# Maxima of the first attention unit from unstacked halves of queries and keys, in 32-row tiles

## The chip, the cores and the metric

The kernel runs on one core of a Trainium2 chip. The metric is the device time of one execution in microseconds (us), lower is better. The times before the change are 1361.73, 1362.64 and 1366.7 us, median 1362.64.

## The reference

Two independent parts, their outputs side by side (448 columns each), sequence length 2048, all in float32. Part A is a state-space convolution (a kernel made of complex exponentials, and a long convolution by Fourier transforms). Part B, which the change touches, is full attention with 16 heads of 28 elements:

```python
qkv = (x @ wqkv).reshape(B, S, 3, H, Dh).transpose(2, 0, 3, 1, 4)
q, k, v = qkv[0], qkv[1], qkv[2]
p = softmax(einsum("bhqd,bhkd->bhqk", q, k) * Dh ** -0.5)
o = einsum("bhqk,bhkd->bhqd", p, v)
return o.transpose(0, 2, 1, 3).reshape(B, S, D) @ wo
```

## The kernel before

**Precision.** TensorE's fast float32 form rounds its operands. So queries, keys, inputs and weights are split in a rounded high half and the rest, hi and lo (`hl` in the names), and a product is the sum of products of halves. Each head is padded from 28 to 32 rows. For the scores, hi and lo are *stacked*: `load_q` (line 162) copies a unit's queries from DRAM into a tile `qhat` with 128 rows, hi, hi, lo, lo; `load_k` (line 143) copies a head's keys into a tile `khat` with hi, lo, hi, lo. One matmul with 128 rows then gives all four products at once.

**Units and maxima.** Attention runs in 16 units, each four heads (a group) by 512 queries. A unit needs the maximum of each query's scores before its exponentials. `max_mm` (line 170) makes, for each of 16 pairs of head and block of 128 queries, four products of 512 keys. The first two blocks of keys are taken as a difference (`kdif`, of the first and second halves of key blocks) and the second halves: max(a, b) = relu(a - b) + b. ScalarE makes the relu (tile `rl`) of the first product, VectorE adds the second and reduces in one instruction, and reduces the third and fourth products alone; all go to the tile `mx`. `max_join`, `max_end` and `max_put` (lines 191 to 206) join them, transpose them, and write them negated as two more rows into the unit's `qhat`, so that score products (`pss`) come out shifted.

**Stages.** In the first stage (about 250 us), 48 projection jobs (`qk_proj`, line 447, and `v_proj`) run among the "seeds" of part A, which load VectorE, ScalarE and POOL (GpSimd); `project` (line 519) takes one job, and the slots of lines 527 to 540 place jobs and the loads named in `ahead`. A projection is 12 matmuls into a PSUM tile `pm` (three of them rotate); its evacuation makes hi on ScalarE and lo on VectorE into a tile `hl` (two rotate), and stores both halves to DRAM (`k<-hl`, `q<-hl`). At the end of that stage the buffers of weights (`w_p`) and inputs (`y_p`) are closed (`wst.close()`), the four `khat` of the first group are loaded into the room, eight of the sixteen loads from ScalarE's queue and eight from SP's, then the second unit's `qhat` and the values `v`, and the maxima of the first unit follow (lines 543 to 548), 64 products into five PSUM tiles. Then comes the long loop. It starts with three steps of the second unit's maxima (`LEAD`, line 860), and goes on with score products, exponentials, products with the values, further maxima, and the rest of part A.

**Order.** In the first stage a scheduler orders the instructions of each engine by its own estimate; from line 857 on the order is that of the program text. Each engine works its list in order; the DMA queue of SP (SyncE) is in order too. Eight DMA semaphores rotate over all transfers, so each transfer is issued only when the one eight places ahead has landed.

Of the kernel before, what the change touches and what calls it, by code (L numbers as in the profile page):

```python
# [17 lines left out]
L = 2048  # L18
D = 448

H = 16
DH = 28
G = 4
HG = H // G
CQ = 512
NQ = L // CQ
NK = L // 128
CK = 112
NCK = D // CK
# [12 lines left out]
SGB, XB, XL = 2, 5, 4  # L42
K0, KP, KD, UP = 0, 3.5, 5, 3
A0, A1 = 26, 34

N1 = 32
N2 = 64
# [43 lines left out]
def body(ctx, tc, a, out):  # L91
    nc = Engines(tc)
# [29 lines left out]
    att, k0_st = ExitStack(), ExitStack()  # L122
# [7 lines left out]
    q_p = pool(att, "q_p", side="right")  # L130
    v_p = pool(att, "v_p", side="right")
    kd_p = pool(att, "kd_p", side="right")

    def mm32(o, w, x_, start, stop, at=0):

# [4 lines left out]

    kt_g, kd_g, q_u, m_u, mh_u, o_u, rl_u = {}, {}, {}, {}, {}, {}, {}

    def load_k(g, j, p, queue=nc.sync):
        t = p.tile([128, L], F32R, name="khat", bufs=HG)
        for r in range(4):
            queue.dma_start(t[32 * r:32 * r + 32, :].bitcast(F32), k_d[g][r % 2, 32 * j:32 * j + 32, :])
        kt_g.setdefault(g, []).append(t)

    v_g = {}
# [19 lines left out]

    def max_mm(u, i, kc, ps=w_tile):  # L170

        if i == 0 and kc == 0:
            m_u[u] = q_p.tile([128, HG, 4, 3], F32, name="mx", bufs=2)
        j, t = divmod(i, 4)
        pm = ps()
        q, kt = q_u[u][:, j, t * 128:(t + 1) * 128], kt_g[u // NQ][j]
        mx = m_u[u][:, j, t, max(kc - 1, 0):max(kc - 1, 0) + 1]
        if kc == 0:
            nc.tensor.matmul(pm, q, kd_g[u // NQ, j], start=True, stop=True)
            rl_u[u, i] = kd_p.tile([128, CQ], F32, name="rl", bufs=2)  # L180
            nc.scalar.activation(rl_u[u, i], pm, AF.Relu)
        elif kc == 1:
            kb = kt.rearrange("p (c s n) -> p c s n", c=NQ, s=2)[:, :2, 1, :]
            nc.tensor.matmul(pm.rearrange("p (c n) -> p c n", c=2), q, kb, start=True, stop=True)
            rl = rl_u.pop((u, i))
            nc.vector.tensor_tensor_reduce(rl, pm, rl, 1.0, -3.0e38, ALU.add, ALU.max, mx)
        else:
            nc.tensor.matmul(pm, q, kt[:, kc * CQ:(kc + 1) * CQ], start=True, stop=True)
            nc.vector.tensor_reduce(mx, pm, axis=AX.X, op=ALU.max)

    def max_join(u):
        m_u[u, 1] = q_p.tile([128, HG * 4], F32, name="m1", bufs=2)
# [16 lines left out]
    with ExitStack() as st:  # L209
# [2 lines left out]
        s_p = pool(sst, "s_p")  # L212
        x_p = pool(xst, "x_p")
        y_p = pool(wst, "y_p", side="right")
        w_p = pool(wst, "w_p", side="right")
        ps_w[0] = pool(st, "ps_w", 1, PSUM)
        ps_t = pool(st, "ps_t", 2, PSUM)
        ps_n = pool(st, "ps_n", 2, PSUM)
# [8 lines left out]
                nc.sync.dma_start(xns[c, h], xs[:, 2 * h:2 * h + 2, :])  # L227

        load_x(0)
        wh = w_p.tile([CK, 2, NCK, H, 32], F32R, name="wh")  # L230
        wl = w_p.tile([CK, 2, NCK, H, 32], F32R, name="wl")
        vh = y_p.tile([CK, NCK, D], F32R, name="vh")
        vl = y_p.tile([CK, NCK, D], F32R, name="vl")
        for w in (wh, wl):
            nc.gpsimd.memset(w[:, :, :, :, DH:].bitcast(F32), 0.0)
# [35 lines left out]
        for k in range(NCK):  # L271
            for s in (1, 0):
                src = wns[k][:, s, :].rearrange("p (h e) -> p h e", e=DH)
                nc.scalar.activation(wh[:, s, k, :, :DH], src, AF.Copy)
                nc.vector.tensor_tensor(wl[:, s, k, :, :DH], src, wh[:, s, k, :, :DH].bitcast(F32), ALU.subtract)
# [171 lines left out]
        def qk_proj(c, s, g):  # L447
            pp = w_tile()
            hs = slice(HG * g, HG * g + HG)
            n = 0  # L450
            for k in range(NCK):
                for w_, x_ in ((wh, xh), (wl, xh), (wh, xl)):
                    nc.tensor.matmul(pp, w_[:, s, k, hs, :].rearrange("p h e -> p (h e)"), x_[k],
                                     start=n == 0, stop=n == 3 * NCK - 1)
# [24 lines left out]

        def v_proj(c, t):  # L480
            pp = w_tile()
            n = 0
            ts = slice(t * 128, (t + 1) * 128)
            for k in range(NCK):
                for w_, x_ in ((vh, xh), (vl, xh), (vh, xl)):
                    nc.tensor.matmul(pp[:, :D], x_[k][:, ts], w_[:, k, :], start=n == 0, stop=n == 3 * NCK - 1)
                    n += 1

            def evac():
                vs = vst[t % 2]  # L490
                nc.scalar.activation(vs[:, :, :DH], pp[:, :D].rearrange("p (h e) -> p h e", e=DH), AF.Copy)
                nc.sync.dma_start(v_d[c][:, :, t], vs.rearrange("p (g h) e -> p g (h e)", g=G))
            return evac

        work = []
# [615 lines left out]
```

## Time and profile before

| | |
|---|---|
| time, median of 3 | 1362.64 us |
| the profiled execution | 1363.72 us |
| its span in the profile | 1361.9 us |
| mean granted TensorE clock | 0.976 |
| instructions | 33142 |
| DMA | 205.36 MB in 200089 packets |

A page of the profile gives the busy time of the engines: PE is TensorE's matmuls, PEld its weight loads, DVE VectorE, ACT ScalarE, POOL GpSimd, SP SyncE; SPq and ACTq are DMA issues. Rows of the time line give start, length, engine, operation and, in brackets, how long the engine stood idle before it and what ended that. Almost every instruction has the line of a helper (L75), so rows are told apart by tile names. Rows of windows give, for a stretch, each engine's busy time with its number of instructions, the granted clock, the busy share of the 16 DMA engines, and GB/s.

### The profile page before, as it was taken

How to read it: one execution, taken by the hardware profiler on the slowest of the kernel's cores; microseconds unless marked ns; L12 is line 12 of the kernel's file. 1: busy time of each engine (PE TensorE's matmuls, PEld its weight loads, DVE VectorE, ACT ScalarE, POOL GpSimd, SP SyncE). 2: the span in 40 equal slices, each digit the busy share in tenths (PEclk: the TensorE clock that was granted, in tenths of full speed). 3: DMA queues.
4: the chain of work that ended last, by engine and by line, in shares of the span. 5: the costliest groups of instructions: out<-in, count | busy, mean ns of one | idle time of the engine just before them, and what ended most of it. 6: DMA issues, size and time to landing. Idle time of an engine off the chain costs nothing.

```text
span 1361.9 us, 33142 instructions
## 1 busy us (share of the span) xinstructions
PE 1243.9 (91%) x12625; PEld 709.8 (52%) x12625; DVE 991.3 (73%) x2138; ACT 966.1 (71%) x2067; POOL 839.5 (62%) x705
## 2 busy tenths in 40 slices
PE   6878885799999999999999999999998999998997
PEld 5657762455555555555555555555555545544433
DVE  5897886877777777777788888888887766857311
ACT  4876752488888888888888887878786655655553
POOL 3685681278877878878888988888895111202221
PEclk9988987899999999999999999999999999999999
DMA  6677669636675545378534233632325534636476
GB/s 197 199 261 266 225 212 271 179 74 150 147 164 118 128 135 159 111 202 198 162 94 97 56 73 86 146 79 67 79 65 140 189 116 161 206 111 203 138 192 176
DMA packets 200089, 205.36 MB, mean 151 GB/s; under 512 B 95993, under 2 KB 158521, under 8 KB 197881
## 3 DMA queue, kind: packets, MB, share of 16 engines
q1 hardware_dynamic: 199544, 201.13, 53.2%
q10 hardware_dynamic: 384, 2.10, 0.6%
q8 instruction: 100, 1.64, 0.5%
q14 instruction: 61, 0.49, 0.1%
HBM read 120.73 MB, written 82.18 MB: 149 GB/s over the span
## 4 chain that ended last, share of the span: by engine, by line
PE 61%; DVE 17%; ACT 12%; issue 3%; DMA 3%; POOL 3%; SPq 0%; ACTq 0%; DVEq 0%; POOLq 0%
PE pm L75 35%; PE po L75 13%; PE pss L75 12%; ACT p L75 6%; DVE mx L75 4%; DVE g L75 2%; DVE tri L75 2%; ACT rl L75 2%; DVE p L75 2%; POOL qhat L75 1%; DVE pr L75 1%; DVE zg L75 1%; DVE rl L75 1%; DVE sg L75 1%; ACT tri L75 1%
## 5 line engine op out<-in xcount | busy, mean ns | idle before, releaser
L75 ACT ACTIVATE p<-pss 128x512 f32<-128x512 f32 x1024 | 565.4, 609 | 138.5 <-PE pss L75 127.5
L75 PE MATMUL pss<-qhat,khat 128*128 128x512 f32 x1024 | 403.1, 400 | 3.3 <-ACT p L75 3.3
L75 DVE TENSOR_REDUCE mx<-pm 128x1 f32<-128x512 f32 x500 | 321.4, 683 | 116.3 <-PE pm L75 115.1
L75 PE MATMUL pm<-khat,qhat 128*128 128x512 f32 x749 | 330.1, 444 | 41.4 <-DVE mx L75 36.5
L75 POOL TENSOR_TENSOR e<-e,sdb 128x256 f32<-128x256 f32 x168 | 201.8, 1201 | 171.9 <-ACT e L75 162.9
L75 PE MATMUL po<-p,v 128*32 128x512 f32 x2048 | 271.9, 599 | 0.0
L75 POOL TENSOR_TENSOR e<-e,eu 128x256 f32<-128x256 f32 x168 | 248.1, 1477 | 13.2
L75 PEld LDWEIGHTS pm<-khat,qhat 128*128 128x128 f32 x749 | 142.0, 190 | 216.0 <-DVE mx L75 79.8
L75 PEld LDWEIGHTS pss<-qhat,khat 128*128 128x128 f32 x1024 | 191.1, 189 | 46.7 <-ACT p L75 11.2
L75 DVE CUSTOM_DVE_ANT_0 rl<-pm,rl 128x512 f32<-128x512 f32 x249 | 171.4, 688 | 48.3 <-ACT rl L75 43.8
L75 POOL TENSOR_TENSOR eu<-e,sdb 128x256 f32<-128x256 f32 x168 | 201.7, 1201 | 0.0
L75 DVE TENSOR_TENSOR g<-g,zg 128x128 f32<-128x128 f32 x392 | 162.9, 416 | 46.3 <-ACT zg L75 41.3
L75 ACT ACTIVATE rl<-pm 128x512 f32<-128x512 f32 x249 | 151.2, 607 | 20.7 <-PE pm L75 18.8
L75 POOL TENSOR_TENSOR p<-pr,pr 64x448 f32<-64x448 f32 x32 | 40.9, 1277 | 191.6 <-DVE pr L75 180.5
L75 PE MATMUL pm<-kdif,qhat 128*128 128x512 f32 x249 | 101.6, 408 | 2.2 <-DVE mx L75 1.5
L75 PEld LDWEIGHTS pm<-e,g 128*32 128x32 f32 x3584 | 63.0, 110 | 52.8 <-issue 30.8
L75 DVE TENSOR_TENSOR zg<-g,zg 128x128 f32<-128x128 f32 x224 | 87.5, 391 | 1.9
L75 PEld LDWEIGHTS po<-p,v 128*32 128x32 f32 x2048 | 56.6, 110 | 42.7 <-issue 38.0
L75 PE MATMUL pm<-xh,wh 112*128 112x512 f32 x128 | 56.8, 448 | 22.3 <-DVE hl L75 10.8
L75 PE MATMUL pm<-e,g 128*32 128x64 f32 x3584 | 72.5, 220 | 0.0
L75 ACT ACTIVATE y<-pm 128x448 f32<-128x448 f32 x48 | 26.3, 548 | 63.0 <-PE pm L75 30.7
L75 DVE TENSOR_TENSOR pr<-pm,ub 128x448 f32<-128x448 f32 x64 | 37.0, 619 | 32.7 <-PE pm L75 32.7
(137 smaller groups left out, 1571.8 us busy)
## 6 DMA issues: line engine op xcount, KB each, us to landing
sdb<-sd SPq DMA_DIRECT2D x56, 336.0 KB
qhat<-q SPq DMA_DIRECT2D x64, 256.0 KB
khat<-k SPq DMA_DIRECT2D x56, 256.0 KB
sd<-sg SPq DMA_DIRECT2D x8, 1456.0 KB
k<-hl SPq DMA_DIRECT2D x16, 512.0 KB
q<-hl SPq DMA_DIRECT2D x16, 512.0 KB
mw<-in_mw SPq DMA_DIRECT2D x16, 512.0 KB
sd<-qhat SPq DMA_DIRECT2D x8, 896.0 KB
```

The lines of the kernel that those rows point to most:

```text
L75: i = f(*args, **kw)
```

## The change

The first unit's maxima no longer use `qhat` and `khat`. Five tiles are loaded straight from DRAM in the form in which the projections stored them, hi and lo side by side and four heads of 32 rows each on the 128 partitions: `own_q` and four blocks of keys (`own_0` the differences, `own_1` the second halves, `own_2` and `own_3`), each 128 x 2 x 512. For each head four matmuls with 32 rows (hi hi, hi lo, lo hi, lo lo) sum into one PSUM tile, at row position 32 j of the array for head j; two heads alternate matmul by matmul. The reading of the products (`max_read`) is as before.

- The loads stand at slots 31, 31, 32, 32 and 34 (`OWN`) of the stage's 41; their room is that of the inputs and of `vh` and `vl`, which is closed after the last values' projections (`own_open`).
- The weights' halves `wh` and `wl` move into four tiles of the `khat` buffers, so that the `khat` loads wait for the last projections tile by tile.
- All sixteen `khat` loads of the first group are now issued by SP.
- The first unit's maxima run by block of queries, pair of heads and block of keys.

```diff
+OWN, KIND, PAIRS = (31, 31, 32, 32, 34), "dbcc", 1
...
+    k0_p = pool(k0_st, "k0_p", side="right")
...
-        wh = w_p.tile([CK, 2, NCK, H, 32], F32R, name="wh")
-        wl = w_p.tile([CK, 2, NCK, H, 32], F32R, name="wl")
+        wh, wl = ([k0_p.tile([128, L], F32R, name="khat", bufs=HG)[:CK].rearrange("p (k h e) -> p k h e", k=NCK, h=H)
+                   for _ in range(2)] for _ in range(2))
...
+        def own_open():
+            wst.close()
+            own_p.append(pool(wst, "own_p", side="right"))
+
+        def own_load(n):
+
+            own[n] = t = own_p[0].tile([128, 2, CQ], F32R, name=f"own_{n}")
+            f = lambda d: d.rearrange("i p l -> p i l")
+            if n == "q":
+                nc.sync.dma_start(t.bitcast(F32), f(q_d[0][0]))
+            elif KIND[n] == "d":
+                nc.sync.dma_start(t.bitcast(F32), f(kd_d[0]))
+            elif KIND[n] == "b":
+                for c in range(2):
+                    c0 = (n - 1 + c) * CQ + CQ // 2
+                    nc.sync.dma_start(t[:, :, c * CQ // 2:(c + 1) * CQ // 2].bitcast(F32), f(k_d[0][:, :, c0:c0 + CQ // 2]))
+            else:
+                nc.sync.dma_start(t.bitcast(F32), f(k_d[0][:, :, n * CQ:(n + 1) * CQ]))
+
+        def own_max(t, js, kc, ps):
+            pms = [p() for p in ps]
+            for n, (a_, b_) in enumerate(((0, 0), (0, 1), (1, 0), (1, 1))):
+                for j, pm in zip(js, pms):
+                    r = slice(32 * j, 32 * j + 32)
+                    nc.tensor.matmul(pm, own["q"][r, a_, t * 128:(t + 1) * 128], own[kc][r, b_, :],
+                                     start=n == 0, stop=n == 3, tile_position=(32 * j, 0))
+            for j, pm in zip(js, pms):
+                max_read(0, 4 * j + t, kc, pm, PAIRS)
...
+            if c == NQ - 1:
+                jobs[0] = (lambda f: lambda: (own_open(), f())[1])(jobs[0])
...
+        for t, n in zip(OWN, ("q", 0, 1, 2, 3)):
+            ahead[t].append(lambda n=n: own_load(n))
...
-                wst.close()
-                k0_p = pool(k0_st, "k0_p", side="right")
                 for j in range(HG):
-                    load_k(0, j, k0_p, nc.scalar if j < 2 else nc.sync)
+                    load_k(0, j, k0_p)
...
-        for i in range(16):
-            for kc in range(4):
-                max_mm(0, i, kc, more[(4 * i + kc) % 5])
+        n_ = 0
+        for t in range(4):
+            for js in ((0, 1), (2, 3)):
+                for kc in range(4):
+                    own_max(t, js, kc, [more[(n_ + i) % 5] for i in range(2)])
+                    n_ += 2
+        wst.close()
```

More of the change, by code (lines that the diff above doesn't have):

```diff
@@ L141, in body, with load_k @@
     kt_g, kd_g, q_u, m_u, mh_u, o_u, rl_u = {}, {}, {}, {}, {}, {}, {}
-    def load_k(g, j, p, queue=nc.sync):
+    def load_k(g, j, p):
         t = p.tile([128, L], F32R, name="khat", bufs=HG)
         for r in range(4):
-            queue.dma_start(t[32 * r:32 * r + 32, :].bitcast(F32), k_d[g][r % 2, 32 * j:32 * j + 32, :])
+            nc.sync.dma_start(t[32 * r:32 * r + 32, :].bitcast(F32), k_d[g][r % 2, 32 * j:32 * j + 32, :])
         kt_g.setdefault(g, []).append(t)
@@ L170, in max_mm @@
     def max_mm(u, i, kc, ps=w_tile):
-        if i == 0 and kc == 0:
-            m_u[u] = q_p.tile([128, HG, 4, 3], F32, name="mx", bufs=2)
         j, t = divmod(i, 4)
@@ L184, in max_mm, with max_read @@
             nc.tensor.matmul(pm.rearrange("p (c n) -> p c n", c=2), q, kb, start=True, stop=True)
-            rl = rl_u.pop((u, i))
-            nc.vector.tensor_tensor_reduce(rl, pm, rl, 1.0, -3.0e38, ALU.add, ALU.max, mx)
         else:
             nc.tensor.matmul(pm, q, kt[:, kc * CQ:(kc + 1) * CQ], start=True, stop=True)
-            nc.vector.tensor_reduce(mx, pm, axis=AX.X, op=ALU.max)
+        max_read(u, i, kc, pm)
+    def max_read(u, i, kc, pm, pairs=1):
+        if u not in m_u:
+            m_u[u] = q_p.tile([128, HG, 4, 4 - pairs], F32, name="mx", bufs=2)
+        j, t = divmod(i, 4)
+        if kc // 2 < pairs and kc % 2 == 0:
+            rl_u[u, i] = kd_p.tile([128, CQ], F32, name="rl", bufs=2)
+            nc.scalar.activation(rl_u[u, i], pm, AF.Relu)
+        elif kc // 2 < pairs:
+            rl = rl_u.pop((u, i))
+            nc.vector.tensor_tensor_reduce(rl, pm, rl, 1.0, -3.0e38, ALU.add, ALU.max, m_u[u][:, j, t, kc // 2:kc // 2 + 1])
+        else:
+            nc.vector.tensor_reduce(m_u[u][:, j, t, kc - pairs:kc - pairs + 1], pm, axis=AX.X, op=ALU.max)
     def max_join(u):
@@ L214, in body @@
         y_p = pool(wst, "y_p", side="right")
-        w_p = pool(wst, "w_p", side="right")
         ps_w[0] = pool(st, "ps_w", 1, PSUM)
@@ L229, in body @@
         load_x(0)
-        wh = w_p.tile([CK, 2, NCK, H, 32], F32R, name="wh")
-        wl = w_p.tile([CK, 2, NCK, H, 32], F32R, name="wl")
+        wh, wl = ([k0_p.tile([128, L], F32R, name="khat", bufs=HG)[:CK].rearrange("p (k h e) -> p k h e", k=NCK, h=H)
+                   for _ in range(2)] for _ in range(2))
         vh = y_p.tile([CK, NCK, D], F32R, name="vh")
         vl = y_p.tile([CK, NCK, D], F32R, name="vl")
-        for w in (wh, wl):
-            nc.gpsimd.memset(w[:, :, :, :, DH:].bitcast(F32), 0.0)
+        for w in wh + wl:
+            nc.gpsimd.memset(w[:, :, :, DH:].bitcast(F32), 0.0)
         vst = [x_p.tile([128, H, 32], F32, name=f"vst{i}") for i in range(2)]
@@ L273, in body @@
                 src = wns[k][:, s, :].rearrange("p (h e) -> p h e", e=DH)
-                nc.scalar.activation(wh[:, s, k, :, :DH], src, AF.Copy)
-                nc.vector.tensor_tensor(wl[:, s, k, :, :DH], src, wh[:, s, k, :, :DH].bitcast(F32), ALU.subtract)
+                nc.scalar.activation(wh[s][:, k, :, :DH], src, AF.Copy)
+                nc.vector.tensor_tensor(wl[s][:, k, :, :DH], src, wh[s][:, k, :, :DH].bitcast(F32), ALU.subtract)
             nc.scalar.activation(vh[:, k, :], wns[k][:, 2, :], AF.Copy)
@@ L452, in qk_proj @@
                 for w_, x_ in ((wh, xh), (wl, xh), (wh, xl)):
-                    nc.tensor.matmul(pp, w_[:, s, k, hs, :].rearrange("p h e -> p (h e)"), x_[k],
+                    nc.tensor.matmul(pp, w_[s][:, k, hs, :].rearrange("p h e -> p (h e)"), x_[k],
                                      start=n == 0, stop=n == 3 * NCK - 1)
@@ L493, in v_proj @@
             return evac
+        own, own_p = {}, []
+        def own_open():
[12 more added lines that the diff above has]
+                    nc.sync.dma_start(t[:, :, c * CQ // 2:(c + 1) * CQ // 2].bitcast(F32), f(k_d[0][:, :, c0:c0 + CQ // 2]))
+            else:
+                nc.sync.dma_start(t.bitcast(F32), f(k_d[0][:, :, n * CQ:(n + 1) * CQ]))
[8 more added lines that the diff above has]
+                max_read(0, 4 * j + t, kc, pm, PAIRS)
         work = []
```

3 lines of the change are left out of this document (removed).

## The prediction

> **What bounds it now.** I read the page first, then the chain of waits between 190 and 262 us, then the time line of the queues there.
>
> ```profile
> span 1361.9 us, 33142 instructions
> PE 1243.9 (91%) x12625; PEld 709.8 (52%) x12625; DVE 991.3 (73%) x2138; ACT 966.1 (71%) x2067; POOL 839.5 (62%) x705
> PE 61%; DVE 17%; ACT 12%; issue 3%; DMA 3%; POOL 3%; SPq 0%; ACTq 0%; DVEq 0%; POOLq 0%
> ```
>
> TensorE is busy 91% of the span and carries 61% of the chain. The change touches none of that; it works on the seam between the projections and the long loop, where the chain is not on TensorE:
>
> ```profile
> 195.38 0.70 DVE hl L75
> ...
> 196.12 7.99 PE pm L75 x24
> 204.11 6.44 DMA khat<-k
> ...
> 210.93 6.78 DMA qhat<-q
> ...
> 228.23 1.21 DVE mx L75 x3
> ...
> 230.04 1.21 DVE mx L75 x3
> ...
> 249.55 1.22 DVE mx L75 x3
> ...
> 250.79 0.21 DVE m L75
> ...
> 252.42 6.14 PE pm L75 x10
> ```
>
> ```profile
> 217.85 0.77 PE L75 MATMUL pt<-kdif,qhat 128*128 128x512 f32 x1 [13.54 <-DMA qhat<-q]
> 257.92 0.34 PEld L75 LDWEIGHTS pss<-qhat,khat 128*128 128x128 f32 x1
> ```
>
> The last projection ends at 204.1; TensorE then stands still for 13.5 us until the stacked queries and keys are in; the 64 maxima products of the first unit run at VectorE's pace, 1.81 us (230.04 less 228.23) for four, until 250.8; three steps of the second unit's maxima follow, and the first score product loads its weights at 257.9. I take that moment as the end of the seam: what it moves by, the end moves by. The seam looks like 13.5 us of waiting plus some 30 us of maxima that could run earlier. But a third thing fills it:
>
> ```profile
> 194.00:196.00 2.00, 0.00 (x0) 0.00 (x0) 1.43 (x2) 2.00 (x3) 0.43 (x1) 0.61 0.01 4
> ...
> 220.00:225.00 5.00, 4.46 (x11) 1.98 (x11) 4.38 (x11) 1.79 (x3) 0.00 (x0) 0.82 1.10 375
> 225.00:230.00 5.00, 4.18 (x12) 1.76 (x11) 5.00 (x13) 1.19 (x2) 0.00 (x0) 1.00 1.04 225
> 230.00:235.00 5.00, 4.38 (x12) 1.91 (x12) 5.00 (x13) 1.79 (x3) 0.00 (x0) 1.00 1.00 210
> ...
> 248.00:250.00 2.00, 0.91 (x3) 0.41 (x3) 2.00 (x5) 0.00 (x0) 0.00 (x0) 1.00 0.14 47
> ```
>
> The last two columns are the busy share of the 16 DMA engines and GB/s. Idle at 194 to 196, they are full from about 200 to 248.3 (0.14 of the last 2 us is 0.3 us). The long loop needs most of what they carry: all four heads' keys, the second unit's queries, and the row of negated maxima that is written into the first unit's queries. So the maxima can be brought forward only as far as this queue lets the loop start.
>
> **The change, step by step.** The times of the queue:
>
> ```profile
> 196.09 0.38 SPq L75 DMA_DIRECT2D q<-hl  x1
> ...
> 199.42 0.38 SPq L75 DMA_DIRECT2D k<-hl  x1
> ...
> 200.74 0.49 SPq L75 DMA_DIRECT2D q<-hl  x1
> ...
> 226.97 3.82 SPq L75 DMA_DIRECT2D qhat<-q  x4
> 231.75 3.83 SPq L75 DMA_DIRECT2D v<-v  x4
> 236.56 0.37 SPq L75 DMA_DIRECT2D sd<-sg  x1
> 237.74 0.37 SPq L75 DMA_DIRECT2D sd<-qhat  x1
> 251.67 1.26 SPq L75 DMA_DIRECT2D qhat<-mh  x2
> ```
>
> An issue waits until the transfer eight places ahead has landed. The eight issues of qhat and v start between 226.97 and 235.3 (231.75 + 3.83 - 0.3), so the eight khat loads before them land 8.3/7 = 1.19 us apart. The two sd stores wait for the first two qhat loads: these land at 236.5 and 237.7, the last of the four at about 240.1, and v and sd end with the queue at 248.3.
>
> 1. The own loads: q, and four blocks of keys, each 128 x 2 x 512 x 4 bytes, 0.52 MB. Bounds by the rates above: 1.4 us each at 375 GB/s, 2.5 us at 210. I take 1.4, since they fill 128 partitions as the sd stores and v do, not 32. Four of them stand in SP's order ahead of the q store of 196.09, behind transfers that end before 194; about 5.6 us of them falls mostly into the idle stretch. The fifth (the last block of keys) stands behind the k store of 199.42 and ahead of the q store of 200.74: +1.4 us for everything after.
>
> 2. The order. Three tiles of the 64 stand ahead of the last projection in the changed program: two before the last but one, one between the two. They cost more by their place than by their work:
>
> ```profile
> 194.76 0.58 ACT L75 ACTIVATE hl<-pm 128x512 fp32r<-128x512 f32 x1
> 195.24 1.32 ACT L75 ACTIVATE tri<-tri,half_pi 128x1232 f32<-128x1232 f32 x1
> ...
> 196.73 1.21 ACT L75 ACTIVATE sg<-sg 128x112 f32<-128x112 f32 x6
> ```
>
> ```profile
> 198.07 0.66 DVE L75 TENSOR_TENSOR sg<-tri 128x336 f32<-128x336 f32 x1
> 198.65 0.74 DVE L75 SCALAR_TENSOR_TENSOR hl<-pm,kones,hl 128x512 fp32r<-128x512 f32 x1
> ...
> 207.73 0.69 DVE L75 TENSOR_TENSOR hl<-pm,hl 128x512 fp32r<-128x512 f32 x1 [0.44 <-ACT hl L75]
> ```
>
> ```profile
> 196.12 0.80 PE L75 MATMUL pm<-xh,wh 112*128 112x512 f32 x1 [3.50 <-DVE hl L75]
> ...
> 200.98 0.54 PE L75 MATMUL pm<-xl,wh 112*128 112x512 f32 x1
> 201.36 0.40 PE L75 MATMUL pm<-xh,wh 112*128 112x512 f32 x1
> ...
> 203.91 0.40 PE L75 MATMUL pm<-xl,wh 112*128 112x512 f32 x1
> ```
>
> The hl of 194.76 (queries of the second group) now stands behind the sine and the six sg copies on ScalarE, and behind sg on VectorE. So its VectorE half ends at about 199.1 (198.07 + 0.66, less the 0.3 by which ScalarE is ahead, + 0.69) and not at 196.1. TensorE waits for that buffer: the last but one projection starts at 199.1. Its 12 matmuls were spaced 0.44 us (4.86/11) after the 3.5 us gap, and the next 12 spaced 0.23 (2.55/11); the gap is now longer, so 5.3 us, to 204.4 (at the faster spacing 2.8 us: the other bound). Then the single own tile, four matmuls of 0.23, to 205.4. VectorE's order has the reduction of that tile, 0.65 us, ahead of the hl of 198.65: this hl ends at 206.9 instead of 199.4. The k store of 199.42 waits for it, and SP's queue is in order: 7.5 us later (5 by the faster spacing), everything behind it the same. Behind it stand the last k and q stores, sd, khat, the second unit's qhat, v, sd, and the negated maxima. This delay is paid from the DMA engines' full stretch, which would otherwise begin at 200.
>
> 3. khat: 16 loads on SP, eight of them formerly on ScalarE's queue. With both queues in work the engines moved 375 GB/s (220 to 225), with khat and qhat alone 210 to 225. Lower bound 0; upper bound the same bytes, eight times 0.26 MB, at 210 instead of 375: 4.4 us. I take 1, near the lower end: the rows from 225 to 235 show that the slow rate belongs to these loads themselves, which fill 32 partitions each. The Trainium skill, "DMA: Bandwidth & Descriptors", section "Issuing engines are not separate DMA queues", says that transfers of all issuing engines run on the same 16 engines, so a second queue would save issue time alone; by that the term is 0 and the sum 1 us lower.
>
> 4. Sum on the queue: 7.5 + 1.4 + 1 = 9.9. The second unit's queries are in at 240.1 + 9.9 = 250.0, and the queue runs out at 258.2. The negated maxima stand on SP behind v and sd. If they land in their turn, about 2 us after the 258.2, it is 260; if the small transfer overtakes, the three steps of the second unit decide, 250.0 + 6.7 (251.2 to 257.9 before) = 256.7. I take the first, as all loads above landed in the order of issue: the first score product at 260, 2 us later than 257.9.
>
> 5. The maxima. VectorE was through with the seeds and the last hl at 208.4 (207.73 + 0.69); now 7.5 us later and with two more reads of maxima ahead of it, about 217. Some 55 tiles remain. VectorE: 55/4 x 1.81 = 25 us, to 242. TensorE: 4 matmuls per tile where one of 128 rows did; if the two tiles of a pair run beside each other, 4 x 0.23 = 0.93 us a pair, 27.5 pairs, 26 us, to 243. Both before 250.0: the 30 us of maxima are hidden behind transfers, and the 13.5 us are spent by the queue. No row here has row tiles. The nearest have column tiles:
>
> ```profile
> L75 PE MATMUL pm<-e,g 128*32 128x64 f32 x3584 | 72.5, 220 | 0.0
> ...
> 175.93 0.71 PE L75 MATMUL pn<-ident,nat 56*128 56x56 f32 x8
> ```
>
> The first: 3584 matmuls of 220 ns in 72.5 us, 20 ns each, so tiles do overlap. The second: eight loads of 128 columns with their matmuls in 0.71 us, 0.09 us each, so eight weight loads a pair are no bound (0.7 under 0.93). I take overlap; none gives 1.86 us a pair.
>
> 6. wh and wl in the keys' buffers: the same casts and matmuls, four fills for two; khat waited for the last projections before too. Nothing, under cover of the first transfers; the fills of POOL are bare otherwise by well under 1 us.
>
> Total +2 us: 1361.9 + 2 = 1363.9 in span; the profiled execution took 1363.72, so 1365.7. It lies 1.1 us above the median of 1362.64, on which the forecast stands: 1364.6, rounded 1365.
>
> **The rivals.** (a) Slower: row tiles don't overlap. From 217 on TensorE then needs 27.5 x 1.86 = 51 us, to 268; three steps 6.7, first score at 275, +17: 1380. The point from which it decides: the maxima must end by about 253 (260 less 6.7), 36 us for 27.5 pairs, 1.3 us a pair; halfway overlap (1.4) costs some 5 us, 1370. For it: no row tile has run here, and four matmuls sum into one buffer. Against: the column tiles above. The Trainium skill, "TensorE: Matmul & The Clock Gate", section "Measured speedup vs the span model", gives 3.07 times for four row tiles of 32 rows and 512 columns; by that a pair would overlap, and rival (a) would not come.
>
> (b) Faster: the delay of step 2 does not come (the reduction finds its tile ready, or the queue never runs empty). Then the second unit's queries are in at 241.5, the maxima end at about 243, the three steps at 250, the negated maxima in their turn at 248.3 + 1.4 + 2 = 251.7: 6 us gained, 8 if they overtake, 1355 to 1357. For it: the DMA engines were idle at 194 to 196, and the own blocks fit there. Against: the order on VectorE is fixed, and the tile it waits for needs a projection that itself waits.
>
> (c) It hardly does what it says: the blocks are loaded among the last projections, but 61 of the 64 tiles stand behind the last one in TensorE's order. That is within the forecast, which gives it no gain.
>
> **How the numbers follow.** Forecast 0.64; (a) 0.20, with its halfway form; (b) 0.13; 0.03 for neither. The forecast's own terms (5 to 7.5, 0 to 4.4, overtaking or not) span -7 to +3 us around it, 1358 to 1368. The range takes in (a) and the weaker half of (b): 1357 to 1381. About 0.5% (6.8 us) is what a measurement of this kernel can tell from no change. Faster by more: half of (b) and a little, 0.08. Slower by more: (a), and 0.06 for terms of the forecast that exceed my bounds, 0.26. Within: 0.66.
>
> **What would show it.** Step 2: the last but one projection starts near 199, the k store of the third group near 207, and the DMA engines have a second idle stretch just before. Step 4: the second unit's first maximum waits for a qhat load near 250, and the first score product near 260 for the negated maxima, with VectorE idle. Step 5: own matmuls in pairs 0.23 us apart per pair of matmuls and maxima over by 245; if they are 0.23 apart each and end near 268, (a) is right. If the first score product comes before 253, the queue was not the bound and my step 2 is wrong.

## The result, and the profile after

| | median us | runs | ratio to before, 95% interval |
|---|---|---|---|
| before | 1363.58 | 4 (1361.73 to 1366.7) | |
| after | 1380.25 | 4 (1378.8 to 1382.26) | 1.0131 [1.0104, 1.0159] |

The change costs 17 us. The forecast was 1365; the time is the one that rival (a) gave, 1380, but not by rival (a)'s mechanism.

The page of the changed kernel: the span, the busy times, and the shares of the chain by engine.

```profile
span 1378.6 us, 33547 instructions
PE 1269.4 (92%) x12817; PEld 735.9 (53%) x12817; DVE 992.6 (72%) x2138; ACT 965.3 (70%) x2067; POOL 839.4 (61%) x707
PE 64%; DVE 16%; ACT 12%; issue 3%; POOL 3%; DMA 2%; SPq 0%; ACTq 0%; DVEq 0%; POOLq 0%
```

TensorE is busy 25.5 us longer (1269.4 less 1243.9), and its share of the chain went from 61 to 64%; VectorE and ScalarE do what they did. The first score product in the time line of TensorE's weight loads:

```profile
275.25 0.32 PEld L76 LDWEIGHTS pss<-qhat,khat 128*128 128x128 f32 x1
```

257.92 became 275.25, 17.3 us later. What follows took 1104.0 us before (1361.9 less 257.92) and 1103.4 after (1378.6 less 275.25). So the whole loss lies ahead of the loop, in the seam. (In the kernels of the experiments the part behind the first score product took 1100.5 to 1108.3 in their profiled executions, so a few us there tell nothing.) Its chain of waits in the changed kernel:

```profile
216.64 2.09 PE pm L76 x4
...
244.22 0.42 PE pt L76
...
245.07 0.42 PE pt L76
...
267.81 0.21 DVE m L76
...
268.45 7.42 PE pm L76 x13
```

The 13.5 us of DMA wait and the stretch in which VectorE set the pace are gone from the chain; from 219.5 to 266.5 it lies nearly all on TensorE. The same stretch by windows (busy us of PE, PEld, DVE, ACT, POOL; then the granted clock, the DMA engines' share and GB/s):

```profile
220.00:225.00 5.00, 4.57 (x23) 2.72 (x19) 1.89 (x3) 0.60 (x1) 0.00 (x0) 0.50 0.99 356
...
235.00:240.00 5.00, 5.00 (x32) 3.88 (x30) 3.04 (x7) 1.08 (x2) 0.00 (x0) 0.50 1.08 226
...
255.00:260.00 5.00, 5.00 (x32) 3.79 (x30) 3.46 (x8) 1.09 (x2) 0.00 (x0) 0.50 0.89 312
260.00:265.00 5.00, 5.00 (x31) 3.78 (x27) 3.04 (x8) 1.08 (x2) 0.00 (x0) 0.50 0.01 3
```

Before, 225 to 240 stood at clock 1.00. After, TensorE is busy all of the time from 230 to 265, and the clock is 0.50 throughout. The DMA engines run empty before 261; the maxima still run to 267.8.

### The profile page after: what moved, and what is told of

It reads as the page before. It is cut to its first block, busy times and chain, and to the rows that moved or that the text cites. A ratio compares the mean times of both kernels' runs of the same rounds, so it can differ in the third digit from the quotient of the medians.

```text
span 1378.6 us, 33547 instructions
## 1 busy us (share of the span) xinstructions
PE 1269.4 (92%) x12817; PEld 735.9 (53%) x12817; DVE 992.6 (72%) x2138; ACT 965.3 (70%) x2067; POOL 839.4 (61%) x707
## 4 chain that ended last, share of the span: by engine, by line
PE 64%; DVE 16%; ACT 12%; issue 3%; POOL 3%; DMA 2%; SPq 0%; ACTq 0%; DVEq 0%; POOLq 0%
PE pm L76 38%; PE po L76 13%; PE pss L76 12%; ACT p L76 6%; DVE mx L76 3%; DVE g L76 2%; DVE tri L76 2%; ACT rl L76 2%; DVE p L76 2%; PE pt L76 2%; POOL qhat L76 1%; DVE pr L76 1%; DVE sg L76 1%; DVE zg L76 1%; ACT tri L76 1%
## 5 line engine op out<-in xcount | busy, mean ns | idle before, releaser
L76 PE MATMUL pm<-khat,qhat 128*128 128x512 f32 x720 | 317.2, 442 | 39.8 <-DVE mx L76 35.4
L76 PEld LDWEIGHTS pm<-khat,qhat 128*128 128x128 f32 x720 | 135.9, 189 | 210.1 <-DVE mx L76 77.0
L76 PEld LDWEIGHTS pss<-qhat,khat 128*128 128x128 f32 x1024 | 190.9, 189 | 46.5 <-issue 11.1
L76 PE MATMUL pm<-xh,khat 112*128 112x512 f32 x256 | 93.8, 450 | 26.2 <-DVE hl L76 14.2
L76 PE MATMUL pm<-kdif,qhat 128*128 128x512 f32 x240 | 96.8, 403 | 0.5 <-DVE pr L76 0.2
L76 PEld LDWEIGHTS pm<-xh,khat 112*128 112x128 f32 x256 | 54.0, 216 | 42.5 <-DVE hl L76 16.4
```

The costliest lines, as they stand in the source:

```text
L76: i = f(*args, **kw)
```

## The experiments

The disputed point is the clock. Is it low because two row groups of 32 rows are half of the array, because the pairs wait now and then, because matmuls of 32 rows never raise it, or because it was low when they began?

Executions differ by some 4 us ahead of the seam (last section), so the table measures each seam within its own profiled execution: from the k store that stands at 149.64 in before to the first score product's weight load. Each ratio is to runs of before on the same chip, whose medians were 1362.46 to 1363.67 (1363.58 for after's).

| kernel | k store | first score | seam | median us | ratio, 95% interval |
|---|---|---|---|---|---|
| before | 149.64 | 257.92 | 108.3 | | |
| after | 149.59 | 275.25 | 125.7 | 1380.25 | 1.0131 [1.0104, 1.0159] |
| warm_free | 150.00 | 267.86 | 117.9 | 1373.69 | 1.0083 [1.0059, 1.0108] |
| pairs_kept | 145.47 | 264.83 | 119.4 | 1374.15 | 1.0079 [1.0054, 1.0105] |
| dummies_kept | 146.18 | 259.24 | 113.1 | 1369.46 | 1.0048 [1.0032, 1.0064] |
| dummies_once | 146.03 | 254.48 | 108.5 | 1365.24 | 1.002 [1.0005, 1.0034] |
| warm_kept | 148.97 | 257.25 | 108.3 | 1363.17 | 1.0008 [0.9997, 1.0019] |
| late_sd | 147.25 | 257.07 | 109.8 | 1363.89 | 1.0008 [0.9993, 1.0024] |
| quads_kept | 149.69 | 260.71 | 111.0 | 1366.59 | 1.002 [1.0004, 1.0037] |
| warm_six | 148.30 | 254.15 | 105.9 | 1358.84 | 0.9975 [0.996, 0.999] |
| six_late | 149.35 | 255.95 | 106.6 | 1363.25 | 0.9993 [0.9977, 1.001] |
| before_six | 145.72 | 251.67 | 106.0 | 1361.77 | 0.9988 [0.9967, 1.001] |

### Streams by themselves: streams and streams_low

```
        for i in range(N):                               # N = 96
            for j, p in enumerate(places):
                r = slice(p, p + rows)
...
                    keep(nc.tensor.matmul(ts[j], x[r, :128], x[r], start=True, stop=True, tile_position=(p, 0)))
...
    stream("one", 32, (0,))                              # name, rows, places
    stream("two", 32, (0, 32))
...
    stream("four", 32, (0, 32, 64, 96))
```

> It leaves the whole computation out (the output is zeros) and runs dense streams of matmuls of 512 columns on fixed data, 96 steps each, with 64 matmuls of 128 rows ahead of each: 32 rows alone, two, three and four row tiles of 32 side by side, 64 rows alone, two of 64 side by side, 96 rows, 128 rows by 32 columns, and two row tiles of 32 with one matmul of 128 rows a step. Theory (half the array): the clock follows how many of the 128 rows work; two row tiles fall to 0.50 however dense they are, so a step of two takes 0.43 us as in the changed kernel, and four, or two of 64, stay at 1.00 with 0.21 to 0.23 us a step. Rival (waits): the pairs of the changed kernel were at 0.50 because each pair waits a little for a buffer; dense pairs here keep 1.00 and take 0.21 to 0.23 us a step. Rival (short rows): a matmul of 32 rows never holds the clock up, so four side by side are at 0.50 too, 0.43 us a step. No overlap at all would give 0.21 us for each matmul: 0.43 for two and 0.85 for four at clock 1.00.

Windows of the first streams: 32 rows alone, two row tiles, four row tiles, 64 rows alone, and the mixed steps.

```profile
32.00:56.00 24.00, 24.00 (x58) 18.53 (x57) 0.00 (x0) 0.00 (x0) 0.00 (x0) 0.50 0.00 0
78.00:94.00 16.00, 16.00 (x144) 14.21 (x142) 0.00 (x0) 0.00 (x0) 0.00 (x0) 1.00 0.00 1
...
152.00:168.00 16.00, 16.00 (x292) 14.18 (x288) 0.00 (x0) 0.00 (x0) 0.00 (x0) 1.00 0.01 2
189.00:205.00 16.00, 16.00 (x73) 12.97 (x72) 0.00 (x0) 0.00 (x0) 0.00 (x0) 1.00 0.00 1
...
340.00:466.00 126.00, 126.00 (x262) 49.80 (x262) 0.00 (x0) 0.00 (x0) 0.00 (x0) 0.50 0.00 0
```

Row tiles overlap in full: two took 142 weight loads in 16 us, 71 steps of 0.225 us; four took 288, 72 steps of 0.22, all at clock 1.00. That is the 0.23 a step that the forecast assumed. But "half the array" is refuted as I had put it: the two dense row tiles, and 64 rows alone, stayed at 1.00. So is "short rows", by the four; "waits" was still open.

These streams all began at the high clock; the pairs of the changed kernel began at the low one. Next, each stream behind 64 matmuls of 32 rows alone, which bring the clock down:

> It leaves the whole computation out, as the first streams did. Each stream now starts from the low clock: 64 matmuls of 32 rows alone stand ahead of it, which took the clock to 0.50 in the first streams. The theory formed from those (work done): the clock is kept or raised where the rows at work, times the share of full-clock time, are above a bound between 0.40 (mixed steps: 192 rows in 0.85 us, 0.227 us a matmul, fell) and 0.50 (two row tiles dense at 1.00, stayed); at the low clock the same stream does half as much. So from 0.50: 128 rows, four of 32, two of 64 and 128 rows by 32 columns do 0.50 and rise to 1.00; two of 32 and 64 rows alone (0.25), three of 32 and 96 rows (0.375) stay at 0.50 for the whole stream; 112 rows (0.44) tells the bound closer. Rival (rows alone): a share of rows of one half or more raises the clock whatever it is, so two, three, 64 and 96 rows rise as well; then the changed kernel's pairs were low for their waits. Rival (history alone): nothing but the full 128 rows raises it. From the high clock, the last three: 56 rows (0.44), 48 (0.375), 40 (0.31): by the first theory 40 falls within some 5 us, and the first that stays gives the bound from above.

Windows of the streams that began low: 96 rows, 64 rows alone, two row tiles, three row tiles; then of those that began high: 56 rows and 48 rows.

```profile
136.00:150.00 14.00, 14.00 (x63) 11.59 (x63) 0.00 (x0) 0.00 (x0) 0.00 (x0) 1.00 0.01 1
180.00:215.00 35.00, 35.00 (x83) 26.83 (x83) 0.00 (x0) 0.00 (x0) 0.00 (x0) 0.50 0.00 0
248.00:284.00 36.00, 36.00 (x172) 27.46 (x170) 0.00 (x0) 0.00 (x0) 0.00 (x0) 0.50 0.00 0
320.00:335.00 15.00, 15.00 (x204) 14.43 (x201) 0.00 (x0) 0.00 (x0) 0.00 (x0) 1.00 0.01 2
...
498.00:514.00 16.00, 16.00 (x72) 12.99 (x71) 0.00 (x0) 0.00 (x0) 0.00 (x0) 1.00 0.00 1
540.00:568.00 28.00, 28.00 (x67) 21.36 (x67) 0.00 (x0) 0.00 (x0) 0.00 (x0) 0.50 0.00 1
```

Two dense row tiles and 64 rows alone never left 0.50, in over 40 us each, without a single wait. "Waits" falls: half of the array keeps a high clock and does not raise a low one. My "work done" falls too, in its form of one bound: three row tiles and 96 rows, which do 0.375 of full work at the low clock, rose to 1.00, while mixed steps doing 0.40 at the high clock lost it. What these streams leave is a bound that depends on the clock found: up from 0.50 with somewhere between 64 and 96 of 128 rows, kept at 1.00 down to somewhere between 56 and 48. (The 56 rows were watched for the 22 us of their stream; 48 had fallen after 4.)

### The maxima behind the last projection, with and without idle matmuls

pairs_kept undoes step 2 alone; dummies_kept adds to it two matmuls a step in the idle row groups:

```
+        nc.kept = KEPT["a"]                                  # pairs_kept: program order from here on
...
+            idle = [j for j in range(4) if j not in js]      # dummies_kept
+            pns = [ps_n.tile([128, CQ], F32, name="pn") for _ in idle]
...
-                for j, pm in zip(js, pms):
+                for j, pm in zip([*js, *idle], pms + pns):
```

> The maxima stay behind the last projection, in program order, so the delay of the forecast's step 2 is undone: the last but one projection starts near 196, not 198.9, the third group's k store near 199.5 to 201, not 207.05, VectorE is through with hl near 208. All theories here: khat and the second unit's queries come some 7 us earlier (last qhat near 243, queue empty near 254). Half the array, and short rows: the clock stays at 0.50 while the pairs run, 32 pairs of 1.71 us from 208 end near 263, first score product near 270, about 1375 us, 5 less than the changed kernel. Rival (waits, or the gap ahead of the maxima of 212.8 to 216.6 as the cause of the low clock): with the gap gone the clock comes up, pairs take 0.93 us, VectorE's pace of 1.9 us for four sets it, the maxima end near 240, first score product near 255, about 1360.

> As the one before, and each pair's matmuls have two more beside them in the two row groups that would stand idle, into buffers that nobody reads: twice the matmuls for the same maxima. Half the array: the clock comes up to 1.00 while the maxima run, a pair takes 0.93 us with its dummies, VectorE sets the pace (64 tiles at 1.9 us for four, 31 us from 208, to 240), the first score product stands near 255, about 1360 us: twice the work, 15 us less than without the dummies. Short rows: the clock stays at 0.50 and nothing changes, 1375. If four row tiles do not overlap fully, slower than 1375.

pairs_kept: 0.50 throughout the pairs, 1374.15 where 1375 was expected, the seam 6.3 us shorter than the changed kernel's. The delay was undone only in part: moved by 4.17 us, the distance of the k stores of the table, the last but one projection starts at 198.0 (193.82 in its own time) where 196 was expected, and the third group's k store stands at 202.7 (198.51) where 199.5 to 201 was. dummies_kept does twice the matmuls and its seam is another 6.3 us shorter, at 1369.46 where 1360 was expected. The window of 230 to 235 us of pairs_kept:

```profile
230.00:235.00 5.00, 5.00 (x32) 3.88 (x30) 3.23 (x8) 1.08 (x2) 0.00 (x0) 0.50 0.99 218
```

The same window of dummies_kept:

```profile
230.00:235.00 5.00, 5.00 (x68) 3.53 (x68) 3.71 (x9) 1.09 (x2) 0.00 (x0) 1.00 1.04 226
```

Two weight loads of dummies_kept that open a pair, in the time line:

```profile
227.22 0.23 PEld L76 LDWEIGHTS pn<-own,own_q 32*128 32x128 f32 x2 [0.44 <-PE pn L76]
...
228.47 0.23 PEld L76 LDWEIGHTS pn<-own,own_q 32*128 32x128 f32 x2 [0.42 <-PE pn L76]
```

The clock is up, as expected, but the pairs are 1.25 us apart (228.47 less 227.22), not 0.93: each waits for the idle matmuls' buffer of the pair before. That is an artefact of the experiment, so the next kernel takes that buffer once for four pairs, and another has idle matmuls beside the first 12 pairs only:

```
-            pns = [ps_n.tile([128, CQ], F32, name="pn") for _ in idle]
+            if beside and kc == 0:
+                own_pn[:] = [ps_n.tile([128, CQ], F32, name="pn") for _ in range(2)]
...
-                    own_max(t, js, kc, [more[(n_ + i) % 5] for i in range(2)])
+                    own_max(t, js, kc, [more[(n_ + i) % 5] for i in range(2)],
+                            (2 - js[0], 3 - js[0]))                       # dummies_once
...
+                            (2 - js[0], 3 - js[0]) if n_ < 24 else ())    # warm_kept
```

> As the pairs kept behind the last projection with two idle matmuls beside each pair, but the buffers of the idle ones are taken once for four pairs and not for each, since each pair there waited 0.33 us for them (pairs 1.25 us apart, not 0.93). Work done: clock 1.00 from about 216 on, pairs 0.93 to 0.95 us apart, VectorE with little idle, maxima over near 242 (252 before), the negated maxima behind the sd stores in the queue, which runs empty near 252: first score product near 253, about 1363, 6 less than with the waits and 11 less than without the idle matmuls. If the clock has nothing to do with the rows at work, no better than 1369.

> The idle matmuls beside the first 12 pairs alone; the other 20 pairs run with two row groups, as in the changed kernel, but start at the high clock. Work done: pairs at 1.00 do 0.50 x 0.93/0.95 = 0.49 of full work, above the bound if that is lower: the clock stays at 1.00 without the idle matmuls and the time is that of the kernel with all of them, about 1363; the changed kernel would then have lost its time by finding the clock low, not by its pairs being unable to hold it. If the bound is at 0.50 or the pairs' waits add up, the clock falls within 5 to 10 us of the 12th pair and the rest takes 1.71 us a pair: first score product near 264, about 1372.

dummies_once came to 1365.24 where 1363 was expected, with the seam at 108.5. warm_kept decides. Its windows: the idle matmuls run to about 225, and the plain pairs follow.

```profile
210.00:215.00 5.00, 2.41 (x19) 1.51 (x23) 2.66 (x6) 1.62 (x4) 0.80 (x1) 0.59 1.06 336
215.00:220.00 5.00, 5.00 (x62) 4.04 (x62) 2.58 (x4) 0.68 (x2) 0.00 (x0) 0.73 1.08 378
...
230.00:235.00 5.00, 4.97 (x40) 3.34 (x36) 4.42 (x11) 1.08 (x2) 0.00 (x0) 1.00 1.04 236
...
240.00:245.00 5.00, 4.97 (x40) 3.12 (x37) 4.43 (x11) 1.32 (x3) 0.00 (x0) 1.00 1.06 235
```

The same pairs that ran at 0.50 from 219.5 to 266.9 in the changed kernel stay at 1.00 here once they find it so, with VectorE busy 4.4 of 5 us. Of every four pairs the first is read by two relus on ScalarE, so the distance of these rows is the time of four pairs:

```profile
236.19 1.08 ACT L76 ACTIVATE rl<-pt 128x512 f32<-128x512 f32 x2 [3.20 <-PE pt L76]
240.48 1.08 ACT L76 ACTIVATE rl<-pm 128x512 f32<-128x512 f32 x2 [3.20 <-PE pm L76]
```

Four pairs take 4.29 us, 1.07 a pair. The seam is 11.1 us shorter than that of pairs_kept for twelve times eight idle matmuls, and equal to that of before. The time matches too: 1363.17 where 1363 was expected.

### The changed kernel in its own order, with the clock lifted: warm_free

The same idle matmuls in the changed kernel itself, without the line that keeps the order.

> The changed kernel in its own order (not kept behind the last projection), with idle matmuls beside the first 12 pairs of the program and nothing else: the clock is lifted, all other parts of the change stay. If the clock is the whole miss, the forecast's own sum holds here: bulk of the maxima from about 217, clock 1.00 some 4 us later, pairs at VectorE's pace, maxima over near 248, three steps and the negated maxima in their turn behind the queue that runs empty near 261: first score product near 262 in place of 275, about 1366 us, 14 less than the changed kernel. If the idle matmuls come to stand apart from the pairs, so that less than four row groups work, the clock stays at 0.50 and the time near 1380. If another part of the change costs as well, it lies between.

It lies between, at 1373.69. Two of its windows:

```profile
225.00:230.00 5.00, 4.85 (x28) 3.18 (x31) 1.85 (x3) 0.01 (x1) 0.00 (x0) 0.50 0.87 238
...
245.00:250.00 5.00, 4.97 (x42) 3.43 (x40) 4.43 (x11) 1.08 (x2) 0.00 (x0) 1.00 1.02 205
```

In the scheduler's order the idle matmuls stood partly apart from their pairs, and the clock came up only after 230, not 221. From there the maxima ran at VectorE's pace. 7.8 of the 17.4 us came back. That the forecast's 1366 would be reached with a clock that is up from 217 on is not shown by this run. Two things lie between the changed kernel and warm_kept, the clock and the place of the maxima. Moving them behind the last projection brings 6.3 us (pairs_kept), and the clock after that 11.1; the clock first brings 7.8, and the place after that 9.6. So the clock is the larger part of the loss and not all of it.

### Four row groups of real work: quads_kept

```
+        more += [lambda: ps_n.tile([128, CQ], F32, name="pn")] * 2 + [lambda: ps_x.tile([128, CQ], F32, name="px")]
...
-                    own_max(t, js, kc, [more[(n_ + i) % 5] for i in range(2)])
+                own_max(t, range(4), kc, [more[(n_ + i) % 8] for i in range(4)])
```

> All four heads' tiles are made at once, in four row groups, with eight PSUM buffers for five (those of the seeds are free by then), behind the last projection in program order. Half the array: the clock comes up to 1.00 while the maxima run unless their pauses (0.9 us of work in each 1.9) bring it down; VectorE sets the pace, maxima over near 240, last qhat of the second unit near 243, first score product near 250 to 255, about 1355 to 1360, below the kernel before. Short rows: the clock stays at 0.50, four tiles take 1.71 us, just under VectorE's 1.9, so the time is the same within 3 us and only the clock tells.

The time was missed, 1366.59, and the clock was that of neither theory. Two windows:

```profile
225.00:230.00 5.00, 4.56 (x40) 2.38 (x34) 3.83 (x10) 2.06 (x4) 0.00 (x0) 1.00 1.01 236
...
235.00:240.00 5.00, 4.93 (x45) 3.58 (x46) 3.25 (x10) 1.31 (x3) 0.00 (x0) 0.62 1.00 229
```

It rose and fell again. The sixteen fours ran from 216.98 to the negated maxima's issue at 254.26, 2.3 us each, of which 0.9 us is work at full clock: 0.39 of the array, below what the streams kept. VectorE's pauses, which the expectation named, are enough to explain it; the run doesn't prove it.

### What is late next: late_sd, warm_six, before_six, six_late

late_sd is dummies_once with the last two sd stores issued behind the negated maxima (in its expectation, "milliseconds" should read microseconds). warm_six is warm_kept with a sixth buffer, before_six the kernel before with the same buffer, six_late both edits:

```
+        more.insert(2, lambda: ps_x.tile([128, CQ], F32, name="px"))        # % 6 in place of % 5
...
+                if o == NO - 1 and i >= len(stages[o]) - 2:                 # late_sd, six_late
+                    late += st_
...
         max_put(0)
+        for f in late:
+            f()
```

> As dummies_once, and the last two sd stores are issued behind the negated maxima and not ahead of them. Theory (queue, step 4 of the forecast): the negated maxima land in their turn, so without the sd stores ahead they land near 246 instead of 252 to 254; the three steps of the second unit's maxima then end last, near 249: first score product near 250, about 1360. If small transfers overtake, no difference to dummies_once. In the first milliseconds of the loop the sd stores fall into a stretch where the engines are idle, so nothing is given back.

> As the kernel with 12 warmed pairs in kept order, and a sixth PSUM buffer for the pairs (the one of the seeds), so that the second pair has not to wait for a buffer that the last projection holds until VectorE's hl. Its seam there: pairs stop from 208.8 to 210.9 and from 212.8 to 214.7, the clock falls to 0.59, and VectorE idles 5 of 15 us between 205 and 220. If these waits are what keeps the maxima from ending sooner, the clock is up 2 to 3 us sooner, first score product 2 to 4 us sooner, about 1360, a little under the kernel before. If VectorE's own order (the hl after the first reads) holds them, no difference: 1363.

> The kernel before, with the sixth PSUM buffer for the first unit's maxima and nothing else. It tells whose gain that of warm_six is. If it is the change's (maxima that need not wait for the stacked queries and keys, once the clock is up and the buffers are there), the sixth buffer alone does nothing here, because VectorE is busy all of the time from 225 to 240 and waits for no buffer: 1362 to 1364. If it is the buffer's, 1359 here too.

> As warm_six, and the last two sd stores are issued behind the negated maxima. In warm_six the negated maxima, issued at 246.46, landed at 253.7, right behind the second sd store (253.5): in their turn, as the forecast's step 4 had it, and the first score product, at 254.15, came just behind them. Without the sd stores ahead they land near 249 to 250; the three steps of the second unit's maxima end last then, at 253: first score product 0.5 to 1 us sooner, 1358, which a run can hardly tell from warm_six. If the three steps are not the next bound, up to 4 us: 1355.

late_sd gained nothing over dummies_once (1363.89 and 1365.24, with intervals that overlap). In both, the first score product follows on the three steps of the second unit's maxima without a wait, so the queue was not what ended their seams, and a shorter queue could not help. warm_six is the only version whose interval lies below 1: 0.9975 [0.996, 0.999]. A window of it:

```profile
235.00:240.00 5.00, 5.00 (x52) 3.65 (x49) 5.00 (x14) 1.08 (x2) 0.00 (x0) 1.00 1.00 220
```

The issue of its negated maxima in the queue's time line:

```profile
246.46 1.28 SPq L76 DMA_DIRECT2D qhat<-mh  x2
```

Its first score product in the time line of the weight loads:

```profile
254.15 0.29 PEld L76 LDWEIGHTS pss<-qhat,khat 128*128 128x128 f32 x1 [1.13 <-DMA sdb<-sd]
```

VectorE is now full, 5.00 of 5, and the score product waits 1.13 us for a transfer. By the semaphores in the trace that is the negated maxima: they land at 253.6 and 253.9, right behind the second sd store, which lands at 253.4. But the same buffer in the kernel before, which I expected to do nothing, shortened the seam as much (106.0 against 105.9). Its time, 0.9988 [0.9967, 1.001], can be told neither from before nor from warm_six. So how much of warm_six's gain is the change's and how much the buffer's stays open.

six_late gained nothing on warm_six: its ratio is 0.9993 [0.9977, 1.001], though the two intervals overlap. A row of its TensorE, in the first steps of the loop:

```profile
262.99 0.80 PE L76 MATMUL pm<-khat,qhat 128*128 128x512 f32 x1 [2.84 <-DVE mx L76]
```

The seam is 0.7 us longer than that of warm_six, not shorter, and then TensorE stands still for 2.84 us (0.35 at the same place in warm_six, 1.46 in warm_kept). The delayed stores are carried while the loop's first loads are due: the engines' share is 1.00 at 255 to 260 and 0.90 at 260 to 265, against 0.77 and 0.77 in warm_six. That the stores cause the stop is argued, not shown.

## Why the prediction was wrong

**Step 1, right as far as the q store shows it.** The four own loads push the k store of 189.62 to 192.46, but not the q store behind it. That one stands at 198.91 in place of 196.09, and it goes out just as VectorE's half of its hl ends (198.21 + 0.68). ScalarE comes to this hl behind the sine and the sg copies, as step 2 had it. In pairs_kept, where no own tile stands ahead, the same store is still 1.9 us late by the k store's measure (193.79 + 4.17 is 197.96), again just behind its hl (193.09 + 0.68). So a part of this delay comes from an order that the scheduler changed without the tiles ahead; why it did was not tried.

**Step 2, right.** The last but one projection of the changed kernel in TensorE's time line:

```profile
198.94 1.22 PE L76 MATMUL pm<-xh,khat 112*128 112x512 f32 x2 [5.24 <-DVE hl L76]
```

Its queue's time line, for this step and the next two:

```profile
207.05 0.39 SPq L76 DMA_DIRECT2D k<-hl  x1
...
223.45 13.11 SPq L76 DMA_DIRECT2D khat<-k  x16
237.57 3.82 SPq L76 DMA_DIRECT2D qhat<-q  x4
...
268.80 1.26 SPq L76 DMA_DIRECT2D qhat<-mh  x2
```

198.94 against a forecast 199.1, waiting for the hl as said; 207.05 against 206.9. Undoing it as far as pairs_kept does brought 6.3 us, though with the maxima as the bound and not the queue.

**Steps 3 and 4, right as far as they were tried.** The second unit's queries are issued 10.6 us later than before (237.57 less 226.97), where 9.9 was forecast, and the engines ran empty before 261, where 258.2 was. That small transfers land in their turn agrees with warm_six, where the negated maxima go out at 246.46 and land 7 us later, just behind the second sd store. But in the changed kernel the queue had long been empty when the negated maxima came at 268.80: step 4 was not what ended the seam. Step 3 alone was not tried.

**Step 5 failed, in the price of a pair.** Row tiles overlap, as I took it: 0.225 us a step for two, against 0.23. But I priced the step at the full clock, since the windows of before had 1.00 in that stretch. Those were matmuls of 128 rows. The pairs of 64 rows came after TensorE's pause (212.8 to 216.6), found the clock at 0.50, and could not raise it: 0.425 us a step (245.07 less 244.22, halved). The pace of the pairs in the changed kernel, from its relus:

```profile
243.83 1.08 ACT L76 ACTIVATE rl<-pm 128x512 f32<-128x512 f32 x2 [4.76 <-PE pm L76]
249.67 1.09 ACT L76 ACTIVATE rl<-pt 128x512 f32<-128x512 f32 x2 [4.76 <-PE pt L76]
```

Four pairs take 5.84 us, 1.46 a pair where I had 0.93. (It is less than four steps, 1.70, because where the pairs change from heads 0 and 1 to heads 2 and 3, or back, the next pair starts beside the last.) The forecast had the last maximum at 243; the last own matmul ends at 266.9. Of these 24 us the price of a pair makes 16: 59 tiles, 29.5 pairs, were left at 219.5, and 29.5 x (1.46 - 0.93) is 15.6. At warm_kept's 1.07 a pair, 11.5 of the 16 are the clock's, and 4 are not, since even at 1.00 a pair takes longer than I had it. The other 8 are a start 2.5 us later than 217, four more tiles than my 55, and slow first pairs: eleven tiles took from 219.5 to about 230.4, 3 us more than at 1.46 a pair, with TensorE waiting for VectorE's reads. What part of these waits is again the low clock's was not separated.

Up to 253 the maxima would have cost nothing, as the point at rival (a) had it. They were joined at 267.8 (the row of m in the chain), 15 us beyond that; from there the first score product came 7.4 us later, before 7.1 (257.92 less 250.79). That is the miss of 15 (275.25 for 260). The shape of the tile changed three things at once, rows, overlap and clock, and I asked only for the second.

**Rival (a)** had the time right, 1380, and the cause wrong. Two matmuls of a pair start together in the changed kernel itself:

```profile
238.17 0.62 PE L76 MATMUL pm<-own,own_q 32*128 32x512 f32 x1
238.17 0.62 PE L76 MATMUL pt<-own,own_q 32*128 32x512 f32 x1
238.59 0.62 PE L76 MATMUL pm<-own,own_q 32*128 32x512 f32 x1
238.60 0.62 PE L76 MATMUL pt<-own,own_q 32*128 32x512 f32 x1
```

Half the clock and no overlap both double a step, so the rival's price came near; that its time was met is luck all the same. It had 27.5 pairs of 1.86 us from 217, to 268; there were 29.5, most of 1.46, from 219.5, to 266.9. Its halfway form had the price nearly right, 1.4, for another reason, and so 1370 (its own sum, 217 + 38.5 + 6.7, ends 4.3 us behind 257.9 and gives 1367). The time alone would have confirmed rival (a); the starts of the matmuls, the granted clock and the streams refute it.

The Trainium skill, "TensorE: Matmul & The Clock Gate", section "What's actually happening", lets the clock rise after about 3.4 us of sustained work on TensorE. Where it rose here that agrees (96 rows had it some 4 us after they began, three row tiles some 5); but two row tiles worked without a pause for over 40 us and had not risen, and the page does not say how many rows must work. The measurement decides.

**Step 6** showed nothing against it, and was not tried by itself.

## What to carry to other kernels

Before splitting a matmul of 128 rows into row tiles, read the granted clock at the place where they will start, and count the rows that work at a time: half of the array keeps a high clock but does not raise a low one, and then each step costs nearly double however dense it is (0.425 us for 0.225). If the work must start behind a pause, let its first part use all row groups, even with matmuls that nobody reads; the 12 pairs of warm_kept were enough. When a rival's time is met to the microsecond, check its mechanism by a second row before believing it, and count the instructions behind a sum that comes out right.

## What the runs showed of the hardware

- The clock has a memory (streams_low, dense matmuls of 512 columns). Up from 0.50: 128, 112 and 96 rows, three or four row tiles, two of 64 rows, and 128 rows by 32 columns rise, all within 4 to 5.5 us; 64 rows and two row tiles of 32 don't, in over 40 us. From 1.00: 56 rows keep it for their 22 us, 48 and 40 have lost it after some 4.
- Row tiles and matmuls of 128 rows didn't overlap each other. In the mixed steps the pair of row tiles overlaps, and then each change of shape takes 0.43 us at the full clock, where a step of either kind by itself takes 0.22 to 0.23. The start of them in TensorE's time line:

```profile
331.21 0.50 PE L69 MATMUL mixed_a<-x 32*128 32x512 f32 x1
331.21 0.50 PE L69 MATMUL mixed_b<-x 32*128 32x512 f32 x1
331.64 0.49 PE L70 MATMUL mixed_c<-x 128*128 128x512 f32 x1
332.06 0.50 PE L69 MATMUL mixed_a<-x 32*128 32x512 f32 x1
```

- Executions differ by several us ahead of the seam, and the granted clock differs with them in a stretch that the change doesn't touch; which of the two causes the other is not shown. The window of 80 to 120 us of before:

```profile
80.00:120.00 40.00, 30.02 (x105) 24.19 (x106) 32.86 (x58) 29.70 (x62) 29.14 (x34) 0.79 0.67 223
```

The same of pairs_kept, whose k store stands 4.2 us earlier:

```profile
80.00:120.00 40.00, 32.48 (x126) 25.75 (x127) 33.82 (x59) 29.07 (x63) 28.64 (x34) 0.84 0.67 225
```
